# The last attention group of layer one: V's key block 7 in a bank of its own, and V, W_o and the first MLP load cut differently

## The chip, the core and the metric

The kernel runs on one core of one Trainium2 chip. The metric is the device time of one execution in microseconds; the median of three runs of the kernel before is 745.25 us (742.36 to 746.46). A core has a matrix engine (PE, with its weight loads shown as PEld), a vector engine (DVE), a scalar engine (ACT), GpSimd (POOL) and a sync engine (SP), which here only issues the loads. Matrix products are written to PSUM; everything else lies in SBUF, in 128 partitions.

## The reference

Two decoder layers, alternating attention and MLP, are run twice with the same weights on a batch of 4 with one token each, D = 640, all in f32:

```python
x = x + _A_ref(_layernorm(x), k_cache, v_cache, wq, wo)
x = x + _B_ref(_layernorm(x), W_gate, W_up, W_down)
x = x + _A_ref(_layernorm(x), k_cache, v_cache, wq, wo)
x = x + _B_ref(_layernorm(x), W_gate, W_up, W_down)
```

`_A_ref` takes 32 heads of 128, the last W = 1024 keys of the cache, and computes softmax(q k^T / sqrt(128)) v and then the product with wo. `_B_ref` computes (relu(x W_gate) * (x W_up)) W_down with F = 1728. Each batch row has its own K and V, so nearly all of the work is reading them.

## The kernel before

All weights and both caches lie in one HBM tensor, `stream`, of 128 partitions, in the order in which the first layer uses them. SBUF holds one large tile, `store`, of 55,040 columns of 4 bytes. One column of a load is 128 x 4 = 512 bytes. The list `todo` names the loads in order, with their sizes; `load()` goes through it, and puts a load on SP's queue as soon as the program has reached the point where the columns that it overwrites have been read for the last time. So the sizes in `todo` set both how much has to land before the matrix engine may go on, and how early the next load can be put into the freed place.

The 32 heads go in 8 groups of 4. For a group, `scores` (L272) multiplies q with K into the tile `ps` (two banks, four batch rows at partitions 0, 32, 64, 96), `softmax` (L279, L281) writes `probs`, `turned` (L296, L297) turns these into `pT`, and `values` (L305) multiplies `pT` with V into `po`. V is laid out by key block: 8 blocks of 128 keys, and for each block 4 heads of 512 columns (4 batch rows of 128). In `po`, head h has partitions 32h to 32h+3, each row b with the product of its probabilities with every batch row's V; only the piece where both are the same row is wanted. ACT copies `po` to `gates` (L308), four small matrix products (L314) turn the wanted pieces into `ms`, DVE scales them to `oT` (L317), and `project` (L325) multiplies with the group's rows of W_o into `yy`, which also gathers the residual.

Usually the turning and projecting of a group is done while the next group's K is landing. After the last group of a layer there is no next group: the turn, the projection, the layer norm (`normalized`, L201 to L220), and the first gate products of the MLP (`gate(3)`, L377) stand one behind the other. The layer norm's variance goes on beside these products.

The last group's K, V and W_o of layer one, group 7, are kept in SBUF for layer two, which starts with that group. While they are kept, the loads of layer one's MLP have only the last 6,912 columns of `store` to go round in (`RING`, from column `KEPT`). The first 6,528 of them (the first five MLP loads) fill places that earlier groups have long left. The sixth, and every one after it, waits until the matrix engine has read the place that it goes to: the sixth, 1,024 columns, for the first MLP load of 1,152 columns, which is the first 9 of the 15 steps of `gate(3)`.

`warm` is a product whose result is not read; it only keeps the matrix engine at work. The code before calls it twice during the last softmax, once after the last block of V, and between the MLP's products.

Of the kernel before, what the change touches and what calls it, by code (L numbers as in the profile page):

```python
# [12 lines left out]
B, D, H, DH, W, F = 4, 640, 32, 128, 1024, 1728  # L13
P = 128
# [7 lines left out]
GH = 4  # L22
G = H // GH
WQ, KV, WO = KC * GH * P, GH * 4096, GH * D
# [3 lines left out]
WD0 = GU0 + 3 * GU  # L28
TAIL, WD1, WD = WD0 + D, WD0 + D + 2 * QUARTER, 4 * D
# [3 lines left out]
AT = {}  # L33
# [21 lines left out]
M0 = AT["mlp"]  # L55
# [4 lines left out]
FRONT = VKEPT + WO  # L60
# [7 lines left out]
def decode_kernel(ctx: ExitStack, tc: tile.TileContext, x, stream, sel, out):  # L68
    nc = tc.nc
# [26 lines left out]
    run(0, AT["q", 7], AT["q", 7] + WQ, place=FRONT)  # L96
    run(0, AT["v", 6], vsplit)
    run(0, vsplit, AT["k", 7], place=0)
    steps(0, AT["k", 7], *[4096] * 7, 2048, 1024, 1024, 1280, 1280, place=FRONT + WQ)
    todo.append([KEPT])  # L100
    steps(0, M0, 9 * P, 6 * P, *[1536] * 3, 1024, 768, *[1536] * 5, 1280, WD1 - WD0, 2 * D, 3 * D, 3 * D, 2 * D, D, D)
    steps(1, AT["q", 6], 512, 1536, 512)
    steps(1, AT["k", 6], 2048, 2048)
    todo.append([FRONT, 0])
# [42 lines left out]
    def get(layer, lo, n):  # L147
        for first, m, p in held[layer]:
            if first <= lo and lo + n <= first + m:
                return store[:, p + lo - first:p + lo - first + n]  # L150
        raise KeyError((layer, lo, n))

    def done(layer, lo, n):
        if layer == 0 and any(a <= lo < b for a, b in kept):
            return
        for first, m, p in held[layer]:
            a, b = max(lo, first) - first, min(lo + n, first + m) - first
            if a < b:
                live[p + a:p + b] = [False] * (b - a)
        load()  # L160
# [4 lines left out]
    probs = work.tile([P, W], F32, name="probs")  # L165
    gates = work.tile([P, 512], F32, name="gates")
# [14 lines left out]
    po = psum.tile([P, 512], F32, name="po")  # L181
# [52 lines left out]
    def warm(moving=None):  # L234

        m = ident if moving is None else moving
        t = ps_p.tile([P, 512], F32, tag="p", name="unread")
        nc.tensor.matmul(t[:, :m.shape[-1]], ident, m, start=True, stop=True)  # L238
# [58 lines left out]
            nc.vector.tensor_copy(t[:, 4 * j:4 * j + 4], pp.rearrange("p c (b r) -> p c r b", r=32)[:, :, :GH, :])  # L297
        return t

    def values(layer, g, t, last):  # L300

        for c in range(8):
            for h in range(GH):
                lo = AT["v", g] + (c * GH + h) * 512
                nc.tensor.matmul(po[32 * h:32 * h + B], t[:, c, h], get(layer, lo, 512),  # L305
                                 start=c == 0, stop=c == 7, tile_position=(0, 32 * h))
                done(layer, lo, 512)
        nc.scalar.copy(gates, po)  # L308
        if last:
            warm(probs[:, :256])  # L310

    def values_turned(r):
        for b in range(B):
            nc.tensor.matmul(ms[:, b * GH:b * GH + GH], gates[:, b * P:(b + 1) * P], ident[:, b:P:32],  # L314
                             start=True, stop=True)
        oT = small.tile([P, GH, B], F32, name="oT")
        nc.vector.tensor_tensor(oT, ms[:, :GH * B].rearrange("p (b h) -> p h b", h=GH),  # L317
                                r.rearrange("p (h b) -> p h b", b=B), op=ALU.mult)
        return oT

    def project(layer, g, oT, last):
        for h in range(GH):
            for q in range(4):
                lo = AT["o", g] + h * D
                nc.tensor.matmul(y[32 * q:32 * q + B], oT[:, h], get(layer, lo + q * QUARTER, QUARTER),  # L325
                                 start=False, stop=last and h == GH - 1, tile_position=(0, 32 * q))
            done(layer, lo, D)

    def attention(layer, gs):
        load()  # L330
        xT, d = normalized()
        rs = []
        query(layer, gs[0], xT, lambda: rs.append(deviation(d)))
        rstd = rs[0]
        table(AF.Exp)
        query_out(rstd)
        query_turned()
        before = None
        for g, after in zip(gs, gs[1:] + [None]):
            scores(layer, g, 0)  # L340
            if before is None:
                go_on()
            else:
                project(layer, before, values_turned(r), False)
            for h in range(1, GH):
                scores(layer, g, h)
            sums = softmax()
            if after is not None:
                query(layer, after, xT)
                query_out(rstd)  # L350
# [9 lines left out]
            values(layer, g, t, layer == 0 and after is None)  # L360
            before = g
        project(layer, before, values_turned(r), True)


    def forward(layer):
# [135 lines left out]
```

## Time and profile before

| what | value |
|---|---|
| median of three runs | 745.25 us (742.36 to 746.46) |
| profiled execution, its own time | 742.0 us |
| its span, first to last instruction | 740.2 us |
| mean granted clock of the matrix engine | 0.808 |
| read from HBM | 312.37 MB, 422 GB/s over the span |
| matrix products, busy | 487.1 us of 740.2 |
| vector engine, scalar engine, busy | 59.0 us, 42.2 us |
| loads on SP's queue | 104 |

The times of the table's first row are without a profile; the profiled execution is one more. The span leaves out 1.8 us before and after the program's own instructions. The busy time of an engine is an average over all stages; which of them matters has to be read from the stretch around the change, which lies at about 340 to 380 us of the span.

### The profile page before, as it was taken

The page shows a single profiled execution, that of the slowest core. Times are in us where ns is not written, and L with a number is a line of the kernel's source. Part 1 is how long each engine was busy: PE and PEld are TensorE (multiplying, and loading weights), DVE is VectorE, ACT ScalarE, POOL GpSimd, SP SyncE. Part 2 cuts the span into 40 slices and gives each one's busy share as a digit, 9 for nine tenths or more (in the row PEclk, how much of TensorE's full clock was granted, in tenths as well). Part 3 has the DMA queues.
Part 4 walks back from the last instruction along what each step waited for, and adds up shares of the span by engine and source line. Part 5 has one row for each costly group of instructions (what it writes and reads, how often), then busy time and mean ns, then how long its engine had stood idle before and what let it go on. Part 6 is the DMA issues. An engine that isn't in the chain of part 4 may idle for free.

```text
span 740.2 us, 8264 instructions
## 1 busy us (share of the span) xinstructions
PE 487.1 (66%) x3844; PEld 158.5 (21%) x3844; DVE 59.0 (8%) x159; ACT 42.2 (6%) x74; POOL 0.2 (0%) x4
## 2 busy tenths in 40 slices
PE   3657376655855565767687997555666587576595
PEld 1112112212211121312233232111122022222142
DVE  2000100101010010101001110101001000010110
ACT  2000000000000000001001000000000000000100
POOL 0000000000000000000000000000000000000000
PEclk9978687876787777878999999778868678698777
DMA  9999999999999999999999999999999999999996
GB/s 388 425 452 437 414 438 433 420 453 414 447 424 427 444 418 416 443 419 425 412 377 402 425 438 426 429 421 443 428 431 437 427 438 429 427 432 433 406 429 284
DMA packets 15306, 312.99 MB, mean 423 GB/s; under 512 B 1700, under 2 KB 1956, under 8 KB 6824
## 3 DMA queue, kind: packets, MB, share of 16 engines
q1 hardware_dynamic: 15120, 312.37, 99.0%
q8 instruction: 30, 0.49, 0.3%
q10 hardware_dynamic: 152, 0.09, 0.0%
q14 instruction: 4, 0.03, 0.0%
HBM read 312.37 MB, written 0.08 MB: 422 GB/s over the span
## 4 chain that ended last, share of the span: by engine, by line
DMA 78%; PE 18%; another core or an unknown queue 2%; DVE 1%; issue 0%; SPq 0%; ACT 0%; ACTq 0%
DMA store<-in_stream 78%; PE ps L272 6%; PE po L305 4%; PE yy L325 2%; PE ms L314 2%; PE qp L252 1%; PE ms L263 1%; PE pp L296 0%; PE qp L377 0%; PE po L377 0%; SPq L143 0%; PE yy L409 0%; PE unread L238 0%; DVE oT L317 0%
## 5 line engine op out<-in xcount | busy, mean ns | idle before, releaser
L272 PE MATMUL ps<-store,qz 128*4 128x512 f32 x1024 | 168.3, 717 | 97.1 <-DMA store<-in_stream 96.6
L305 PE MATMUL po<-store,pT 128*4 128x512 f32 x1024 | 163.6, 745 | 83.7 <-DMA store<-in_stream 83.7
L272 PEld LDWEIGHTS ps<-store,qz 128*4 128x4 f32 x1024 | 30.7, 96 | 205.0 <-issue 112.3
L305 PEld LDWEIGHTS po<-store,pT 128*4 128x4 f32 x1024 | 28.5, 98 | 199.6 <-issue 110.0
L252 PE MATMUL qp<-store,xT 128*4 128x512 f32 x160 | 41.1, 760 | 26.7 <-DMA store<-in_stream 26.6
L281 ACT ACTIVATE probs<-ps,nm 128x1024 f32<-128x1024 f32 x16 | 17.8, 1113 | 308.7 <-DVE nm L279 308.7
L279 DVE TENSOR_REDUCE nm<-ps 128x1 f32<-128x1024 f32 x16 | 19.6, 1225 | 191.1 <-PE ps L272 191.1
L317 DVE TENSOR_TENSOR oT<-ms,r 128x16 f32<-128x16 f32 x16 | 2.8, 174 | 346.0 <-PE ms L314 346.0
L325 PE MATMUL yy<-store,oT 128*4 128x160 f32 x512 | 25.5, 351 | 4.3 <-DVE oT L317 4.3
L308 ACT COPY gates<-po 128x512 f32<-128x512 f32 x16 | 9.4, 585 | 309.3 <-PE po L305 309.3
L314 PEld LDWEIGHTS ms<-sel_sb,gates 128*128 128x128 f32 x128 | 18.7, 225 | 19.0 <-issue 16.8
L377 PE MATMUL po<-store,xT 128*4 128x256 f32 x160 | 17.2, 495 | 6.3 <-DMA store<-in_stream 6.1
L314 PE MATMUL ms<-sel_sb,gates 128*128 128x4 f32 x128 | 20.1, 281 | 0.9 <-ACT gates L308 0.8
L296 PE MATMUL pp<-sel_sb,probs 128*128 128x128 f32 x128 | 19.0, 296 | 0.0
L263 PE MATMUL ms<-sel_sb,gates 128*128 128x4 f32 x128 | 17.3, 258 | 1.7 <-DVE gates L257 1.7
L263 PEld LDWEIGHTS ms<-sel_sb,gates 128*128 128x128 f32 x128 | 17.3, 210 | 4.5 <-DVE gates L257 4.4
L252 PEld LDWEIGHTS qp<-store,xT 128*4 128x4 f32 x160 | 6.4, 96 | 50.4 <-DMA store<-in_stream 30.3
L296 PEld LDWEIGHTS pp<-sel_sb,probs 128*128 128x128 f32 x128 | 17.0, 166 | 0.0
L325 PEld LDWEIGHTS yy<-store,oT 128*4 128x4 f32 x512 | 13.4, 96 | 11.0 <-DVE oT L317 5.7
L285 PE MATMUL ms<-sel_sb,sm 128*128 128x16 f32 x32 | 7.0, 294 | 13.3 <-ACT probs L281 13.3
L257 DVE TENSOR_SCALAR gates<-qp,rstd 128x512 f32<-128x512 f32 x16 | 12.0, 749 | 41.6 <-PE qp L252 41.6
L285 PEld LDWEIGHTS ms<-sel_sb,sm 128*128 128x128 f32 x32 | 5.4, 210 | 31.5 <-ACT probs L281 24.9
(64 smaller groups left out, 115.2 us busy)
## 6 DMA issues: line engine op xcount, KB each, us to landing
store<-in_stream SPq DMA_DIRECT2D x26, 6656.0 KB, 50.2
store<-in_stream SPq DMA_DIRECT2D x11, 2048.0 KB, 32.3
store<-in_stream SPq DMA_DIRECT2D x2, 6784.0 KB, 51.0
store<-in_stream SPq DMA_DIRECT2D x6, 1280.0 KB, 20.7
store<-in_stream SPq DMA_DIRECT2D x7, 1024.0 KB, 8.5
store<-in_stream SPq DMA_DIRECT2D x9, 768.0 KB, 6.9
store<-in_stream SPq DMA_DIRECT2D x1, 6848.0 KB, 47.2
store<-in_stream SPq DMA_DIRECT2D x1, 6720.0 KB, 46.7
```

The source lines that it names most:

```text
L252: nc.tensor.matmul(qp[q:q + B], xT[:, c], get(layer, lo, GH * P), start=c < 4, stop=c > 0, tile_position=(0, q))
L257: nc.vector.tensor_scalar(gates, qp, rstd, SCALE, op0=ALU.mult, op1=ALU.mult)
L263: nc.tensor.matmul(ms[:, h * B:h * B + B], gates[:, h * P:(h + 1) * P], sel_b, start=True, stop=True)
L272: nc.tensor.matmul(ps[32 * b:32 * b + GH, j, :], qz[:, turn[0], b, GH * h:GH * h + GH], get(layer, lo, 512), start=h == 0, stop=h == GH - ...
L279: nc.vector.tensor_reduce(nm, flat, axis=AX.X, op=ALU.max, negate=True)
L281: nc.scalar.activation(probs, flat, AF.Exp, bias=nm, accum_out=sums)
L285: nc.tensor.matmul(ms[:, :GH * B].rearrange("p (h b) -> p h b", b=B), sums.to_broadcast([P, P]), ident_hb, start=True, stop=True)
L296: nc.tensor.transpose(pp[:, c, :], probs[:, (4 * j + c) * P:(4 * j + c + 1) * P], ident)
L305: nc.tensor.matmul(po[32 * h:32 * h + B], t[:, c, h], get(layer, lo, 512), start=c == 0, stop=c == 7, tile_position=(0, 32 * h))
L314: nc.tensor.matmul(ms[:, b * GH:b * GH + GH], gates[:, b * P:(b + 1) * P], ident[:, b:P:32], start=True, stop=True)
L325: nc.tensor.matmul(y[32 * q:32 * q + B], oT[:, h], get(layer, lo + q * QUARTER, QUARTER), start=False, stop=last and h == GH - 1, tile_pos ...
L377: nc.tensor.matmul(gu[32 * g:32 * g + B, :2 * n], xT[:, c], get(layer, lo, 2 * n), start=c == 0, stop=c == KC - 1, tile_position=(0, 32 * g))
```

## The change

Three things are changed, all in layer one's last group and the start of its MLP.

The loads: V's third load of 4,096 columns (key blocks 4 and 5) becomes two of 2,048, the second W_o load of 1,280 columns becomes two of 640 (one head's rows each), and the first two MLP loads of 1,152 and 768 columns become 768 and 1,152. Two later MLP loads of 1,024 and 768, which go round into their places, change order in the same way.

The products with V: `values` does seven of the eight key blocks into `po`. Both halves of `po` are then copied, one by DVE and one by ACT. Key block 7 goes, head by head and batch row by batch row, into the first bank of `ps` (free by then), where row b of each head is at partition 32b, so each product has 128 columns in place of 512. The turn of `po` stands between the block's first two heads and its last two. The heads of block 7 are copied to `probs`, one each by ACT and DVE, and four more turning products add them to `ms`. The unread product after the last V block is gone. The same code serves the other groups and layer two through the old path.

```diff
-    steps(0, AT["k", 7], *[4096] * 7, 2048, 1024, 1024, 1280, 1280, place=FRONT + WQ)
+    steps(0, AT["k", 7], *[4096] * 6, 2048, 2048, 2048, 1024, 1024, 2 * D, D, D, place=FRONT + WQ)
     todo.append([KEPT])
-    steps(0, M0, 9 * P, 6 * P, *[1536] * 3, 1024, 768, *[1536] * 5, 1280, WD1 - WD0, 2 * D, 3 * D, 3 * D, 2 * D, D, D)
+    steps(0, M0, 6 * P, 9 * P, *[1536] * 3, 768, 1024, *[1536] * 5, 1280, WD1 - WD0, 2 * D, 3 * D, 3 * D, 2 * D, D, D)
...
-    def values(layer, g, t, last):
+    def values(layer, g, t, blocks=8):
...
-        nc.scalar.copy(gates, po)
-        if last:
-            warm(probs[:, :256])
+        if blocks < 8:
+            nc.vector.tensor_copy(gates[:, 256:], po[:, 256:])
+            nc.scalar.copy(gates[:, :256], po[:, :256])
+        else:
+            nc.scalar.copy(gates, po)
+
+    def last_values(layer, g, t):
+
+        values(layer, g, t, 7)
+        for hs in (0, 1), (2, 3):
+            for h in hs:
+                lo = AT["v", g] + (7 * GH + h) * 512
+                for b in range(B):
+                    nc.tensor.matmul(ps[32 * b:32 * b + B, 0, h * P:(h + 1) * P], t[:, 7, h],
+                                     get(layer, lo + b * P, P), start=True, stop=True, tile_position=(0, 32 * b))
+                done(layer, lo, 512)
+            for h, copy in zip(hs, (nc.scalar.copy, nc.vector.tensor_copy)):
+                copy(probs[:, h * P:(h + 1) * P], ps[:, 0, h * P:(h + 1) * P])
+            if hs[0] == 0:
+                turn_values(more=True)
...
+    def values_turned(r, last=False):
+        if last:
+            for h in range(GH):
+                nc.tensor.matmul(ms[:, h:GH * B:GH], probs[:, h * P:(h + 1) * P], ident[:, 0:P:33],
+                                 start=False, stop=h == GH - 1)
+        else:
+            turn_values()
```

What the matrix engine executes at this place, from the last group's softmax to the layer norm. Each row is a run of equal products of one line, with the written and read tiles, the columns written, and how many. Before:

```order
L238 MATMUL unread<-gates,sel_sb 128x512 x2
L285 MATMUL ms<-sel_sb,sm 128x16
L296 MATMUL pp<-sel_sb,probs 128x128 x8
L305 MATMUL po<-store,pT 4x512 x32
L238 MATMUL unread<-probs,sel_sb 128x256
L314 MATMUL ms<-sel_sb,gates 128x4 x4
L325 MATMUL yy<-store,oT 4x160 x16
L208 MATMUL xt_ps<-sel_sb,probs 128x16
```

And with the change, where L331 is the old L314, L350 the old L325, L321 the products of key block 7 and L337 their turn:

```order
L238 MATMUL unread<-gates,sel_sb 128x512 x2
L285 MATMUL ms<-sel_sb,sm 128x16
L296 MATMUL pp<-sel_sb,probs 128x128 x8
L305 MATMUL po<-store,pT 4x512 x28
L321 MATMUL ps<-store,pT 4x128 x8
L331 MATMUL ms<-sel_sb,gates 128x4 x4
L321 MATMUL ps<-store,pT 4x128 x8
L337 MATMUL ms<-sel_sb,probs 128x4 x4
L350 MATMUL yy<-store,oT 4x160 x16
L208 MATMUL xt_ps<-sel_sb,probs 128x16
```

The last four of 32 wide products became sixteen narrow ones, the turn of `po` moved ahead of the last eight of them, and a second turn of four products came in behind.

On SP's queue, the loads from group 7's K to the MLP's first half, with their columns. Before:

```order
L143 DMA store<-in_stream 128x4096 x7
L143 DMA store<-in_stream 128x2048
L143 DMA store<-in_stream 128x1024 x2
L143 DMA store<-in_stream 128x1280 x2
L143 DMA store<-in_stream 128x1152
L143 DMA store<-in_stream 128x768
L143 DMA store<-in_stream 128x1536 x3
L143 DMA store<-in_stream 128x1024
L143 DMA store<-in_stream 128x768
L143 DMA store<-in_stream 128x1536 x5
```

With the change:

```order
L143 DMA store<-in_stream 128x4096 x6
L143 DMA store<-in_stream 128x2048 x3
L143 DMA store<-in_stream 128x1024 x2
L143 DMA store<-in_stream 128x1280
L143 DMA store<-in_stream 128x640 x2
L143 DMA store<-in_stream 128x768
L143 DMA store<-in_stream 128x1152
L143 DMA store<-in_stream 128x1536 x3
L143 DMA store<-in_stream 128x768
L143 DMA store<-in_stream 128x1024
L143 DMA store<-in_stream 128x1536 x5
```

There are two loads more, 106 in place of 104, of the same columns in all.

More of the change, by code (lines that the diff above doesn't have):

```diff
@@ L298, in turned @@
         return t
-    def values(layer, g, t, last):
-        for c in range(8):
+    def values(layer, g, t, blocks=8):
+        for c in range(blocks):
             for h in range(GH):
@@ L305, in values, with turn_values @@
                 nc.tensor.matmul(po[32 * h:32 * h + B], t[:, c, h], get(layer, lo, 512),
-                                 start=c == 0, stop=c == 7, tile_position=(0, 32 * h))
+                                 start=c == 0, stop=c == blocks - 1, tile_position=(0, 32 * h))
                 done(layer, lo, 512)
-        nc.scalar.copy(gates, po)
-        if last:
-            warm(probs[:, :256])
-    def values_turned(r):
+        if blocks < 8:
[16 more added lines that the diff above has]
+                turn_values(more=True)
+    def turn_values(more=False):
         for b in range(B):
             nc.tensor.matmul(ms[:, b * GH:b * GH + GH], gates[:, b * P:(b + 1) * P], ident[:, b:P:32],
-                             start=True, stop=True)
+                             start=b == 0, stop=b == B - 1 and not more)
+    def values_turned(r, last=False):
[5 more added lines that the diff above has]
+            turn_values()
         oT = small.tile([P, GH, B], F32, name="oT")
@@ L359, in attention @@
                 query_turned()
-            values(layer, g, t, layer == 0 and after is None)
+            last = layer == 0 and after is None
+            (last_values if last else values)(layer, g, t)
             before = g
-        project(layer, before, values_turned(r), True)
+        project(layer, before, values_turned(r, last), True)
     def forward(layer):
```

## The prediction

> **What bounds the kernel now.** I read the page first, its DMA line and the chain that ended last:
>
> ```profile
> span 740.2 us, 8264 instructions
> DMA  9999999999999999999999999999999999999996
> HBM read 312.37 MB, written 0.08 MB: 422 GB/s over the span
> DMA 78%; PE 18%; another core or an unknown queue 2%; DVE 1%; issue 0%; SPq 0%; ACT 0%; ACTq 0%
> ```
>
> The 16 DMA engines are at 90% or more in all slices but the last, and the chain is loads for 78%. 18% on PE means only that some loads were issued when PE gave a place free; whether the queue ran dry meanwhile must be read from landings. So I looked at the timeline of PE around the change, where a row that waits for a load starts as the load lands:
>
> ```profile
> 338.50 2.54 PE L272 MATMUL ps<-store,qz 128*4 128x512 f32 x16 [2.39 <-DMA store<-in_stream]
> 343.41 3.38 PE L272 MATMUL ps<-store,qz 128*4 128x512 f32 x16 [2.37 <-DMA store<-in_stream]
> 353.21 1.90 PE L305 MATMUL po<-store,pT 128*4 128x512 f32 x16 [0.61 <-DMA store<-in_stream]
> 358.23 1.90 PE L305 MATMUL po<-store,pT 128*4 128x512 f32 x16 [3.12 <-DMA store<-in_stream]
> 360.65 1.04 PE L305 MATMUL po<-store,pT 128*4 128x512 f32 x8 [0.52 <-DMA store<-in_stream]
> 361.93 1.03 PE L305 MATMUL po<-store,pT 128*4 128x512 f32 x4 [0.24 <-DMA store<-in_stream]
> 363.19 1.03 PE L305 MATMUL po<-store,pT 128*4 128x512 f32 x4 [0.24 <-DMA store<-in_stream]
> 364.15 0.70 PE L238 MATMUL unread<-probs,sel_sb 128*128 128x256 f32 x2
> 369.27 1.16 PE L377 MATMUL qp<-store,xT 128*4 128x128 f32 x27
> 372.52 1.03 PE L377 MATMUL po<-store,xT 128*4 128x256 f32 x12 [0.86 <-DMA store<-in_stream]
> 374.43 1.03 PE L377 MATMUL po<-store,xT 128*4 128x256 f32 x12 [0.87 <-DMA store<-in_stream]
> 375.70 0.60 PE L377 MATMUL po<-store,xT 128*4 128x256 f32 x4 [0.24 <-DMA store<-in_stream]
> ```
>
> 4,096 columns take 4.91 us (338.50 to 343.41), 1,024 take 1.26 (361.93 to 363.19). That is (4.91 - 1.26) / 3,072 = 1.19 ns a column and 1.26 - 1.22 = 0.04 us for each load; with the 1.28 from 360.65 to 361.93 in place of 1.26 it is 1.18 ns and 0.07 us. In the MLP, behind the transition, the pace is the same: 1,536 columns in 1.91 us (1.81 + 0.07 = 1.88), then 1,024 in 1.27. So loads land without a gap before, over and behind the transition.
>
> Now the chain there, from V's last landing to the first load that had to wait for PE:
>
> ```profile
> 363.19 1.05 PE po L305 x4
> 364.32 0.59 ACT gates L308
> 364.96 1.07 PE ms L314 x8
> 366.05 0.19 DVE oT L317
> 366.28 1.31 PE yy L325 x32
> 367.68 0.30 ACT probs L201
> 368.02 0.40 PE xt_ps L208 x2
> 369.27 0.85 PE qp L377 x17
> 370.14 5.51 DMA store<-in_stream
> 375.65 0.04 issue
> ```
>
> SP issues the sixth MLP load (1,024 columns) at 370.14 and it lands at 375.65. What would be the earliest? The kernel's first load, on an empty queue, from the list of issues:
>
> ```profile
> store<-in_stream SPq DMA_DIRECT2D x1, 1280.0 KB, 5.6
> ```
>
> 1,280 KB are 2,560 columns, 3.02 us at 1.18 ns, so 2.6 us are latency. The sixth MLP load could have landed at 370.14 + 2.6 + 1.21 = 373.95. It landed 1.7 us later, because it stood behind the loads ahead of it: **the long serial chain has 1.7 us to spare**. One view speaks against this, the windows:
>
> ```profile
> 360.00:370.00 10.00, 8.04 (x103) 3.90 (x102) 1.24 (x6) 0.88 (x2) 0.00 (x0) 1.00 1.02 415
> 370.00:374.00 4.00, 2.64 (x47) 1.07 (x41) 0.44 (x2) 0.57 (x2) 0.00 (x0) 1.00 0.91 335
> 374.00:384.00 10.00, 9.02 (x83) 3.38 (x83) 0.86 (x4) 0.73 (x2) 0.00 (x0) 1.00 1.01 382
> 384.00:394.00 10.00, 8.11 (x96) 3.11 (x93) 0.43 (x2) 0.37 (x1) 0.00 (x0) 1.00 1.02 403
> ```
>
> The last three columns are granted clock, DMA share and GB/s. In 370 to 374 the DMA share is 0.91 and the rate falls from 415 to 335: some of the 16 engines do run dry. But a load has landed only when its slowest engine is done, and the landings above (1.91, 1.27) show no gap. My reading: the engines that are ahead run dry, the one that is behind does not, and it sets the time.
>
> **The change, part by part.**
>
> *Two more loads.* V's blocks 4 and 5 in two, W_o's second load in two: 2 x 0.04 to 0.07 us, +0.1 us, on the path, because the queue is the bound. SP's own time to issue them hides: the chain has SPq at 0%. The Trainium skill, "DMA: Bandwidth & Descriptors", section "Anatomy of one DMA", fits about 2.0 us of fixed cost to each DMA (on the GpSimd path); two more would be an estimated +4.0 us by that, 746.0 in place of 742.1. The landings here show the fixed part overlapped when loads queue behind each other, and I take the row.
>
> *Key block 7.* Before, the last two heads take 1.05 us, ACT's copy 0.59, the turn 1.07. With the change the last two heads are eight products of 128 columns, one quarter of the columns in four groups: the 1.90 us of a full block pair (16 records of 512) divided by 4 is 0.5. From the other side, 27 records of 128 columns (`gate(3)`) took 1.16 us, so 16 take 0.7. I take 0.6. The copies of 128x128 are one each on ACT and DVE; the nearest rows are
>
> ```profile
> L201 ACT COPY probs<-yy x4: 292/292/292, 11.8 to 710.6; 128x160 f32<-128x160 f32 x4
> L297 DVE COPY pT<-pp x32: 160/224/226, 47.4 to 691.4; 128x64 f32<-128x64 f32 x32
> ```
>
> so 0.3 us for the later of the two. Of the second turn's four products the first two run during these copies; the last two cost half of 1.07, 0.5. The turn of `po` (1.07 us) moves ahead, but not for free: block 6 lands at 360.65, is done at 361.7, its two half copies end near 362.1, the first half of block 7 ends about 362.5, the turn then at 363.6, 0.4 us behind V's last landing at 363.2. That is what queues there: the last eight products wait for the turn. So the last products run 363.6 to 364.2, copies to 364.5, turn to 365.1, `oT` and its hand-overs (366.28 - 366.03 = 0.25) to 365.3: the projection may start 1.0 us earlier than 366.28.
>
> *W_o is late next.* Its last columns follow V's by 2,560 columns, 3.0 us, plus three loads' fixed cost: 366.4. Two thirds of the projection and more are done by then; only the last head's four products (a quarter of 1.31, 0.33) follow. It ends at 366.8 in place of 367.6: **0.8 us gained on PE, not 2**. The unread product that is taken out cost nothing: it ran from 364.15 to 364.85, beside ACT's copy.
>
> *The first MLP load of 768 columns.* It is read in 6 of 15 steps, so its place is free after 0.57 in place of 0.85 us. The sixth MLP load is then issued at 370.14 - 0.8 - 0.3 = 369.05, **1.1 us earlier**. It lands behind the same queue as before. Worth on the path: 0 as long as the 1.7 us of cover stand; if the cover had been gone, at most 1.1 us. V's block 4 lands and is read earlier, which is also hidden.
>
> *Engines that run dry later or not at all.* The engines ahead keep up to 1.1 us more of their lead, and a lead is of use when something delays one engine. Such a thing is on the page:
>
> ```profile
> q8 instruction: 30, 0.49, 0.3%
> ```
>
> 30 fetches of instructions are 0.3% of 16 engines' span, 740.2 x 16 x 0.003 / 30 = 1.2 us of one engine each. One or two of them fall in the next 20 us; a kept lead could hide one wholly or not at all, 0 to 1.1 us. MLP loads go round in 6,912 columns (8.2 us), so the lead is cut again within these; I take 0.2. The change adds some 70 instructions to 8,264, a quarter of a fetch by 8,264 / 30 = 275 for each: 0 to +1.2, I take 0.
>
> Sum: +0.1 - 0.2 = -0.1 us on the profiled execution's 742.0 us (span 740.2 and 1.8 around it), which is no change. That execution is 3.25 us under the median of the runs, inside their spread of 4.1. I put the same sum on the median: **745.2 us**. Half a per cent, 3.7 us, is about what a measurement of this kernel can tell from no change.
>
> **The rivals.**
>
> 1. *The dry engines count.* If what all 16 engines move sets the time, the stretch 370 to 394 lacks (415-335)/415 x 4 + (415-382)/415 x 10 + (415-403)/415 x 10 = 1.9 us, and the 1.1 us earlier issue wins back most of its share: 1.1 us, 744.2. For it: the windows. Against: evenly spaced landings. Also within half a per cent.
>
> 2. *The transition stalls in runs without a profile.* The median is 3.25 us over the profiled run, and if all of that were a stall at this place, through a PE clock that fell before the last V blocks, the finer V loads would keep PE at work and take it away with the 1.1 us: 745.25 - 4.3 = 741.0, faster. For it: the clock does fall near here, as in
>
> ```profile
> 340.00:344.00 4.00, 1.63 (x12) 0.11 (x8) 0.00 (x0) 0.00 (x0) 0.00 (x0) 0.50 0.98 418
> ```
>
> and the row at 343.41 takes 3.38 us for what takes 1.90 at full clock. Against: the window 360 to 370 has clock 1.00, and 3.1 us of waiting before 358.23 did not lower it.
>
> 3. *Slower: the clock falls in the MLP.* An unread product is gone, and the products with V are a quarter as wide, so PE does less between 361 and 367. At half clock (3.38 against 1.90, 1.78 times) the chain's 4 us of PE work take 3 us more, and the issue at 369.05 becomes 372.1, past 370.14 + 1.7 = 371.85: from there it decides, with 0.3 us. Then the second and third gate products, 10,240 columns with an unread one behind each 1,024, need 0.55 + 0.42 = 0.97 us for each 1,024 at full clock, by the chain's
>
> ```profile
> 377.10 0.55 PE qp L377 x8
> 377.65 0.42 PE unread L238 x2
> ```
>
> and 1.7 at half, against landings of 1.27: 0.45 x 10 = 4.5 us if the clock stays low through both, with the 0.3 us 4.8 us, about 750; half of it, if the clock recovers midway, 748. Against: the pieces land 1.3 to 2.5 us apart, closer than the 5.0 before (353.21 to 358.23), so PE has no longer pause than now. The Trainium skill, "TensorE: Matmul & The Clock Gate", says the clock is lowered after an idle window of about 3.4 us; by that rule the change makes this less likely, and the 3.1 us pause that kept full clock agrees.
>
> **How the numbers follow.** Hidden, no change, 745.2: 0.62 (744 to 746.4 by the unknown costs). Dry engines count, 744.2: 0.24. Stall removed, 741.0: 0.08. Clock falls, 748 and over: 0.06. Faster by over half a per cent takes the third case and not all of it, slower nearly all of the last: 0.07 and 0.05, within it 0.88. The runs before spread from 742.4 to 746.5 by themselves, more than any term of the sum, so the range takes their spread around 745.2 and stretches to case 3's lower half: 742.0 to 747.8.
>
> **What would show it.** In the changed profile: V's last landing to the next rows' loads at the same spacing (1.9 us for 1,536 columns); the projection's last quarter waiting for W_o, and the layer norm about 0.8 us earlier relative to V's last landing; SP's first waiting MLP load about 1.1 us earlier, its time to landing longer by the same (5.5 to about 6.6) and the landing not earlier; a DMA share in the four microseconds around it nearer to 1.0 than 0.91. I am wrong if landings behind the transition come earlier by as much as the chain does, if PE's granted clock leaves 1.00 between 360 and 394, or if the time moves by more than 3.7 us.

## The result: slower by half a per cent, and the profile after

| | before | after |
|---|---|---|
| median of 22 runs each | 746.54 us (742.36 to 749.1, and one of 970.31) | 750.39 us (743.9 to 754.26) |
| ratio after / before | | 1.0053, 95% interval 1.0032 to 1.0074 |
| profiled execution | 742.0 us, clock 0.808 | 751.56 us, clock 0.801 |

The changed kernel is slower by 3.9 us. The forecast of no change (745.2, 742.0 to 747.8) is wrong, and what came is its third rival. The profiled run of before is faster than every one of its 22 runs, that of after slower than after's median: the two profiles lie 9.5 us apart, the medians 3.9. The first lines of the page after, its DMA line, what it read and its chain:

```profile
span 749.8 us, 8334 instructions
DMA  9999999999999999999999999999999999999996
HBM read 312.37 MB, written 0.08 MB: 417 GB/s over the span
DMA 77%; PE 20%; DVE 1%; another core or an unknown queue 1%; issue 0%; SPq 0%; ACT 0%; ACTq 0%; DVEq 0%
```

The bytes are the same, the rate is 417 GB/s in place of 422, and PE has two points more of the chain. The page does not say where. The windows do: clock, DMA share and GB/s are the last three columns. First before, then after:

```profile
364.00:374.00 10.00, 7.68 (x126) 4.67 (x124) 1.69 (x8) 1.45 (x4) 0.00 (x0) 1.00 0.98 385
374.00:390.00 16.00, 14.73 (x126) 5.38 (x127) 0.86 (x4) 0.73 (x2) 0.00 (x0) 1.00 1.01 389
390.00:405.00 15.00, 11.28 (x168) 5.47 (x168) 2.59 (x10) 2.41 (x5) 0.00 (x0) 1.00 1.02 406
```

```profile
364.00:374.00 10.00, 9.21 (x130) 6.04 (x126) 1.98 (x9) 1.13 (x4) 0.00 (x0) 0.58 0.93 356
374.00:390.00 16.00, 13.33 (x103) 5.19 (x99) 0.86 (x4) 0.74 (x2) 0.00 (x0) 0.73 0.93 342
390.00:405.00 15.00, 11.20 (x134) 4.89 (x130) 0.61 (x3) 0.37 (x1) 0.00 (x0) 0.83 0.96 354
```

Before, PE keeps its full clock through all three stretches. After, it has 0.58, 0.73 and 0.83 of it, and the transfer rate falls with it, from 385 to 356 and from 389 to 342. PE's timeline after, from V's last blocks into the gate products:

```profile
355.74 1.04 PE L305 MATMUL po<-store,pT 128*4 128x512 f32 x8 [0.68 <-DMA store<-in_stream]
358.14 1.04 PE L305 MATMUL po<-store,pT 128*4 128x512 f32 x8 [1.36 <-DMA store<-in_stream]
360.65 1.04 PE L305 MATMUL po<-store,pT 128*4 128x512 f32 x8 [1.48 <-DMA store<-in_stream]
361.92 0.62 PE L321 MATMUL ps<-store,pT 128*4 128x128 f32 x16 [0.22 <-DMA store<-in_stream]
362.72 1.05 PE L331 MATMUL ms<-sel_sb,gates 128*128 128x4 f32 x8 [0.18 <-ACT gates L310]
363.70 0.62 PE L321 MATMUL ps<-store,pT 128*4 128x128 f32 x16
364.25 1.17 PE L337 MATMUL ms<-sel_sb,probs 128*128 128x4 f32 x8
365.68 2.32 PE L350 MATMUL yy<-store,oT 128*4 128x160 f32 x32 [0.27 <-DVE oT L342]
370.11 2.10 PE L403 MATMUL qp<-store,xT 128*4 128x128 f32 x27
372.33 4.09 PE L403 MATMUL po<-store,xT 128*4 128x256 f32 x39
379.84 0.61 PE L403 MATMUL qp<-store,xT 128*4 128x256 f32 x6 [1.13 <-DMA store<-in_stream]
382.94 1.02 PE L403 MATMUL qp<-store,xT 128*4 128x256 f32 x2 [1.54 <-DMA store<-in_stream]
384.62 1.04 PE L403 MATMUL qp<-store,xT 128*4 128x256 f32 x8
385.58 0.80 PE L238 MATMUL unread<-sel_sb 128*128 128x128 f32 x2
386.31 1.03 PE L403 MATMUL qp<-store,xT 128*4 128x256 f32 x8
```

Up to 365.68 all is at full speed: the last eight products start at 363.70 (forecast 363.6), the projection at 365.68 (forecast 365.3, before 366.28). Then the projection takes 2.32 us in place of 1.27, 27 gate products 2.10 in place of 1.16, and the 39 records from 372.33 run as one block of 4.09 with no wait for a load, where before there were three waits: PE is behind the queue now. Later it waits 1.13 and 1.54 us: the queue has run out. The projection before, in the same view:

```profile
366.28 1.27 PE L325 MATMUL yy<-store,oT 128*4 128x160 f32 x32 [0.27 <-DVE oT L317]
```

The list of landings gives the whole loss. From each landing's distance to the one before I take 1.18 ns a column and 0.07 us for the load, and call the rest, where it is over 0.05 us, a gap:

| profiled run | time | gaps, whole span | of them at landings from 365 to 495 us | time less gaps |
|---|---|---|---|---|
| before | 742.0 | 7.3 | 2.4 | 734.7 |
| after | 751.56 | 16.8 | 12.0 | 734.7 |

All of the 9.5 us between the two profiled runs is gaps in 365 to 495, that is the MLP of layer one and the start of layer two. From 340 to 365 there is none over 0.05 us. The same holds for the experiments: time less gaps lies between 734.7 and 735.6 us in all 18 profiled runs.

One of the gaps shows how it comes. SP's first waiting load is issued at 371.19 (before 370.14), still inside its 1.7 us of cover: it lands without a gap. Those behind it are issued up to 2.5 us later than the same columns before (374.24 in place of 371.70), and the engines use up their lead: before, the first of the 16 pieces of the load landing at 376.63 was 2.2 us ahead of the last; after, 0.54 us (the load landing at 376.68). Then the last pieces of two loads come late, 1.55 and 2.75 us behind the first ones, and the two take 6.2 us to land (376.68 to 382.90) in place of 3.8. In that stretch there is a fetch of instructions, at 379.3; the line for it in the DMA queues of after, 370 to 385 us (packets, MB, share of 16 engines):

```profile
q8 instruction: 1, 0.02, 0.4%
```

### The profile page after: what moved, and what is told of

It reads as the page before. It is cut to its first block, busy times and chain, and to the rows that moved or that the text cites. A ratio compares the mean times of both kernels' runs of the same rounds, so it can differ in the third digit from the quotient of the medians.

```text
span 749.8 us, 8334 instructions
## 1 busy us (share of the span) xinstructions
PE 492.2 (66%) x3874; PEld 163.4 (22%) x3874; DVE 60.3 (8%) x162; ACT 42.5 (6%) x76; POOL 0.2 (0%) x4
## 4 chain that ended last, share of the span: by engine, by line
DMA 77%; PE 20%; DVE 1%; another core or an unknown queue 1%; issue 0%; SPq 0%; ACT 0%; ACTq 0%; DVEq 0%
DMA store<-in_stream 77%; PE ps L272 6%; PE po L305 4%; PE yy L350 2%; PE ms L331 2%; PE qp L252 1%; PE unread L238 1%; PE po L403 1%; PE qp L403 1%; PE yy L435 1%; PE ms L263 1%; PE pp L296 1%; SPq L143 0%; DVE oT L342 0%
## 5 line engine op out<-in xcount | busy, mean ns | idle before, releaser
L272 PE MATMUL ps<-store,qz 128*4 128x512 f32 x1024 | 171.3, 732 | 102.9 <-DMA store<-in_stream 102.3
L305 PE MATMUL po<-store,pT 128*4 128x512 f32 x1016 | 158.2, 732 | 78.6 <-DMA store<-in_stream 78.6
L252 PE MATMUL qp<-store,xT 128*4 128x512 f32 x160 | 39.6, 728 | 23.7 <-DMA store<-in_stream 23.6
L350 PE MATMUL yy<-store,oT 128*4 128x160 f32 x512 | 27.6, 372 | 4.3 <-DVE oT L342 4.3
L331 PEld LDWEIGHTS ms<-sel_sb,gates 128*128 128x128 f32 x128 | 20.5, 244 | 20.2 <-issue 18.0
L331 PE MATMUL ms<-sel_sb,gates 128*128 128x4 f32 x128 | 21.9, 295 | 1.0 <-ACT gates L312 0.8
L403 PE MATMUL po<-store,xT 128*4 128x256 f32 x160 | 14.5, 506 | 6.2 <-DMA store<-in_stream 6.2
L350 PEld LDWEIGHTS yy<-store,oT 128*4 128x4 f32 x512 | 13.8, 100 | 12.2 <-DVE oT L342 5.7
L403 PE MATMUL qp<-store,xT 128*4 128x256 f32 (+1 forms) x140 | 11.4, 393 | 5.0 <-DMA store<-in_stream 4.8
```

The costliest lines, as they stand in the source:

```text
L252: nc.tensor.matmul(qp[q:q + B], xT[:, c], get(layer, lo, GH * P), start=c < 4, stop=c > 0, tile_position=(0, q))
L272: nc.tensor.matmul(ps[32 * b:32 * b + GH, j, :], qz[:, turn[0], b, GH * h:GH * h + GH], get(layer, lo, 512), start=h == 0, stop=h == GH - ...
L403: nc.tensor.matmul(gu[32 * g:32 * g + B, :2 * n], xT[:, c], get(layer, lo, 2 * n), start=c == 0, stop=c == KC - 1, tile_position=(0, 32 * g))
```

## The theories

*Clock*: PE's clock falls in the transition or behind it, PE gives places free late, the loads' gaps are the loss. *Fetches*: the 70 instructions more move the fetches to where they hurt. *Loads*: the finer loads cost more than 0.04 to 0.07 us each. And a question inside the first: which edit lets the clock fall, the missing unread product, the narrow products, or the finer V loads?

## The experiments: which part of the change

The first four ran together, and each was timed against before in 12 runs.

**After, with two unread products behind block 7.** They stand ahead of the second turn, where the removed one had been.

```diff
             (last_values if last else values)(layer, g, t)
+            if last:
+                warm()
+                warm()
```

> The changed kernel with two unread 128-column products put back between the last product of key block 7 and its turn (together as many columns as the one that the change took out). Clock theory: PE does so little between 361 and 366 us that its granted clock falls to 0.5 at 365.7, and everything behind it runs at half speed; with the unread products the clock stays 1.00 from 347 to beyond 400, the first waiting MLP load is issued near 370 and no MLP load lands late: ratio to the kernel before 0.998 to 1.002. If two are too little, the clock still falls and the ratio stays near 1.005. Load theory: the two more loads and the other cut make the queue run dry whatever the clock does: still 1.004 to 1.007.

Ratio 1.0054 (1.0032 to 1.0075): nothing is won back. Its profiled run, 748.5 us, does hold the clock in the transition, and so shows the new chain at full speed:

```profile
363.92 0.62 PE L321 MATMUL ps<-store,pT 128*4 128x128 f32 x16
364.47 0.71 PE L238 MATMUL unread<-sel_sb 128*128 128x128 f32 x4
365.02 0.95 PE L337 MATMUL ms<-sel_sb,probs 128*128 128x4 f32 x8
366.24 1.27 PE L350 MATMUL yy<-store,oT 128*4 128x160 f32 x32 [0.27 <-DVE oT L342]
369.23 1.16 PE L406 MATMUL qp<-store,xT 128*4 128x128 f32 x27
```

```profile
369.89 0.33 SPq L143 DMA_DIRECT2D store<-in_stream  x1
```

The unread ones put 0.55 us on the chain (364.47 to 365.02). V's last load landed at 363.40 here, so without them the issue is at 369.89 - 0.55 - 363.40 = 5.94 us behind V; the forecast was 369.05 - 363.15 = 5.90. There is a fetch at 379.7, in the same place as after's, but the two loads that took 6.2 us after take 3.8 here, with leads of 2.2 to 2.8 us; the load behind them is 0.89 us late. The clock, which was expected to hold beyond 400, falls from 397.4 to 404.2, in the down products:

```profile
390.00:405.00 15.00, 11.37 (x144) 5.23 (x136) 1.12 (x5) 0.66 (x2) 0.00 (x0) 0.77 0.92 337
```

and the gaps of 365 to 495 are 8.6 us. So the loss is not tied to one place.

**Before, with the changed loads alone** (the two lines of `steps` of the diff above).

> The kernel before with only the changed loads (V's blocks 4 and 5, W_o and the first MLP loads cut as in the change), products as before with the unread one. Clock theory: the products keep the clock as before, ratio 0.998 to 1.002; if it is the shorter pauses between V's blocks that let the clock fall, about 1.004. Load theory: all of the loss is here, 1.004 to 1.007.

1.0011 (0.9993 to 1.0029). Two more loads at 2.0 us each, the Trainium skill's fixed cost (on the GpSimd path) in "DMA: Bandwidth & Descriptors", section "Anatomy of one DMA", would be an estimated 4.0 us or 1.0054, outside this interval. The loads theory falls as the whole cause.

**Before's loads, after's products.** `last_values` and the second turn as in the diff above (so without the unread product), `steps` as before.

> The changed products (key block 7 in its own bank, its own turn, without the unread product), the loads cut as before. Clock theory: nearly all of the loss is here, 1.003 to 1.007, with the granted clock falling to 0.5 between 361 and 370. Load theory: 0.998 to 1.002.

1.0026 (0.9999 to 1.0054): some of the loss perhaps; not settled by itself.

**Before without its unread product.**

```diff
         nc.scalar.copy(gates, po)
-        if last:
-            warm(probs[:, :256])
```

> The kernel before without the one unread product behind the last block of V, nothing else changed. Clock theory in its narrow form (that product alone kept the clock): 1.003 to 1.006 and a clock that falls near 365. In its wide form (the narrower products matter as much): 1.000 to 1.003. Load theory: 0.999 to 1.001, since nothing about the loads is changed.

1.0009 (0.9987 to 1.0031). Its profiled run, 747.96 us, has half clock from 359.9 to 363.3 and from 366.7 to 373.5, although by its runs the kernel is hardly slower than before. With the first experiment, which put products back and won nothing, the missing product is not shown to be the cause by itself.

## The experiments: fetches or clock

Small unread products (128x4) at the start of the program move all later instructions, and with them the fetches. They also raise the mean clock over the span (0.816 in the first kernel below, before beside it 0.808), so mean clocks of kernels with and without them are not compared here.

```diff
+    t = ps_p.tile([P, 512], F32, tag="p", name="unread")
+    for _ in range(16):
+        nc.tensor.matmul(t[:, :4], ident, ident[:, :4], start=True, stop=True)
     attention(0, list(range(G)))
```

**Before with 16 of them.** The fetch at 384.1 moves to 379.7.

> The kernel before with 16 tiny unread products (128x4) at its start, where PE waits for the first loads. They are 64 more PE instructions, as many as the change adds, so that every later fetch of instructions comes as early in the program as in the changed kernel; nothing else is changed. Fetch theory (the change is slower because a fetch moves from 384 us, between two gate products, to 379.5, where it delays a DMA engine that is already behind): about 1.003 to 1.005, with the fetch near 379.5. Clock theory (what PE streams in each 3.4 us around the last V block and the MLP's start sets the granted clock): 0.999 to 1.001.

0.9991 (0.9970 to 1.0011). **After with its two unread products behind block 7, and 46 small ones:**

> The first experiment (the changed kernel with two unread products put back) with 46 tiny products at the start, so that with its own 72 more instructions the fetches are moved by 256, one whole fetch, and fall where they do in the kernel before (384, not 379.5). Fetch theory: 0.999 to 1.002, and no loss of a load between 380 and 400. Clock theory: unchanged, about 1.005.

1.0038 (1.0014 to 1.0063). **After with 48 small ones and nothing else:**

> The changed kernel with 48 tiny products at the start, so that fetches fall where they do in the kernel before; the unread product behind the last V block stays out. Fetch theory alone: 0.999 to 1.002. Clock theory alone: about 1.005, with a clock of 0.5 within 358 to 372. Both together: 1.002 to 1.004.

1.0033 (1.0007 to 1.0060). Before does not become slower, nor is after shown to be as fast as before, where the fetches lie elsewhere. The profiles say the same of single loads: in before with 16 small products the loads from 376 to 385 us land without a gap over the fetch at 379.7, and in after with 48 one load lands 2.14 us late (377.88 to 381.90) with no fetch from 373.2 to 382.8. So fetches alone are not it; what held up the last pieces in after's two late loads is not shown, and a small part of the time for the fetches is not excluded.

**After with PE kept at work at every wait**: two unread products behind each of V's blocks 3 to 6, four behind block 7, one more place in the down products, and 36 small ones at the start.

```diff
                 done(layer, lo, 512)
+            if blocks < 8 and c > 2:
+                warm()
+                warm()
...
+            if last:
+                warm()
+                warm()
+                warm()
+                warm()
...
-                if layer == 0 and j == 1:
+                if layer == 0 and j < 2:
                     warm()
```

> The changed kernel with more unread products: two behind each of V's blocks 3 to 6, four behind block 7, and one in each step of the MLP's down product that had none, with 36 tiny products at the start so that fetches fall as before. Clock theory: every 3.4 us window from 347 to 400 then streams enough, the granted clock stays 1.00 there, and the ratio is 0.995 to 0.999. If the unread products themselves get in the way of real ones: over 1.002 with the clock at 1.00.

0.9991 (0.9971 to 1.0012), with a mean clock of 0.820 over its runs (0.815 in after with 48 small ones): the loss is gone, with after's loads and after's products. Its interval and after's do not touch. The clock was not held as expected, though: its profiled run, 748.33 us and so one of its slower ones, has 1.00 from 342 to 369.3 and half clock from 369.3 to 372.7 and from 396.6 to 403.5.

## The experiments: the cover, and how wide the unread products must be

**Before, with four more unread products of 512 columns behind the last block of V.** This makes the chain longer, to measure the cover of 1.7 us.

```diff
             warm(probs[:, :256])
+            for _ in range(4):
+                warm(probs[:, :512])
```

> The kernel before with four more unread products of 512 columns behind the last V block: about 3.7 us more on the serial chain, at full clock, since they stream. The prediction's cover (1.7 us between the first waiting MLP load's earliest and its real landing): the load is issued near 373.8 and lands 3.7 - 1.7 = 2.0 us behind its place in the queue; ratio near 1.002. All hidden: no gap. Nothing hidden (the chain is on the path in full): a gap of 3.7 us, ratio 1.005.

1.0044 (1.0026 to 1.0062). SP's first waiting load, and the windows:

```profile
374.29 0.33 SPq L143 DMA_DIRECT2D store<-in_stream  x1
```

```profile
364.00:374.00 10.00, 9.20 (x92) 5.60 (x91) 1.24 (x6) 0.88 (x2) 0.00 (x0) 0.89 0.79 320
```

Relative to V's last landing (363.40 here, 363.15 before) the issue is 3.90 us later, partly because the clock fell here too. The load lands 3.20 us behind the one before it (374.61 to 377.81) where 1,024 columns take 1.28, a gap of 1.92: the cover was 3.90 - 1.92 = 2.0 us. The forecast had 1.7. The ratio is above the 1.002 expected; the clock fell again from 371.8 to 378.6, so the ratio is not the price of the four products alone. Here the DMA engines stand idle for want of a free place, and a share of 0.79 shows it.

**After, with one unread product of 512 columns behind block 7:**

```diff
+            if last:
+                warm(gates)
```

> The changed kernel with one unread product of 512 columns behind key block 7, twice the columns of the one taken out, nothing else. Clock theory with one place (the thin stretch from V's last landing to the projection): clock 1.00 from 347 to 390 and a ratio of 0.999 to 1.002, against 1.005 with 256 columns. If the shorter pauses between V's blocks or the down product matter as much: 1.002 to 1.004.

1.0059 (1.0032 to 1.0086). A wide product there does not help more than two narrow ones, and in its profiled run the clock, expected at 1.00 from 347 to 390, falls from 360.0 to 363.5, from 370.3 to 373.7 and from 383.9 to 387.3. The next two go back to **before's products, with after's loads**, the unread ones behind V's blocks 3 to 6, 512 columns in place of 256 behind block 7, and the additional place in the down products:

```diff
+            if last and 2 < c < 7:
+                warm()
+                warm()
         nc.scalar.copy(gates, po)
         if last:
-            warm(probs[:, :256])
+            warm(probs[:, :512])
...
-                if layer == 0 and j == 1:
+                if layer == 0 and j < 2:
```

> The kernel before with the change's loads and more unread products: two behind each of V's blocks 3 to 6, 512 columns in place of 256 behind block 7, one in each step of the down product that had none. Clock theory: the same as the changed products with unread ones in these places (0.9991), 0.996 to 0.999, which says that block 7's new form costs nothing by itself when the clock holds. If the new form costs time by itself (a second turn, narrow products): lower than that by 0.002 or more.

0.9991 (0.9972 to 1.0009); its profiled run has half clock from 369.1 to 372.5 and from 396.4 to 403.3. **The same with still more of them**, in the down products and behind layer two's first softmax:

> The one before with still more unread products: a second one in every other step of the down product, and two behind the first softmax of layer two, where the clock fell in nearly every profile (396 to 404, 410 to 414). Clock theory: 0.994 to 0.998, and fewer stretches at 0.5 between 395 and 420. If PE is full there: 0.999 to 1.002.

1.0000 (0.9985 to 1.0015). The fastest forms, with either kind of products, are as fast as before and not faster.

## The experiments: which wait matters

The kernel with all unread products had won back everything; these four take it apart. All are after with one or two of the edits shown.

**Only the two behind each of V's blocks 3 to 6:**

> The changed kernel with two unread products behind each of V's blocks 3 to 6 and nothing else. If it is the pauses between V's blocks that let the clock fall: 0.999 to 1.002, clock 1.00 up to 362 at least. If it is the thin stretch from V's last landing to the projection: still 1.003 to 1.006, with a clock that falls between 362 and 371.

1.0012 (0.9995 to 1.0030), below after's interval; its profiled run has full clock from 341.7 to 369.0. **Only the one in the down products:**

> The changed kernel with one unread product in each of the MLP's down steps that had none (one of layer-one's four parts more), nothing else. If what brought the time back before was the down product: 0.999 to 1.002. If it was what stands ahead of the MLP: 1.004 to 1.006.

1.0077 (1.0049 to 1.0106). Its profile shows the chain at half clock nearly from end to end:

```profile
358.23 1.58 PE L305 MATMUL po<-store,pT 128*4 128x512 f32 x8 [1.35 <-DMA store<-in_stream]
360.75 1.89 PE L305 MATMUL po<-store,pT 128*4 128x512 f32 x8 [0.94 <-DMA store<-in_stream]
363.66 1.87 PE L331 MATMUL ms<-sel_sb,gates 128*128 128x4 f32 x8 [0.17 <-ACT gates L310]
366.43 1.87 PE L337 MATMUL ms<-sel_sb,probs 128*128 128x4 f32 x8
368.56 2.31 PE L350 MATMUL yy<-store,oT 128*4 128x160 f32 x32 [0.27 <-DVE oT L342]
```

```profile
374.07 0.33 SPq L143 DMA_DIRECT2D store<-in_stream  x1
```

The clock is 0.5 from 358.6 to 375.7. Ahead of the fall V's pieces were the only work, 1.04 us in each 2.5. Both turns take 1.87 us. The first waiting load is issued 10.8 us behind V's last landing (before 7.0), past the cover, with a gap of 1.78 us at its landing.

**The ones behind V's blocks and one of 512 columns behind block 7:**

> The changed kernel with two unread products behind each of V's blocks 3 to 6 and one of 512 columns behind block 7. If V's pauses and the thin stretch act together: 0.997 to 1.001, clock 1.00 from 347 to 369 at least. If the down product's unread ones were needed too: 1.002 to 1.004.

1.0024 (1.0004 to 1.0045): by its twelve runs a part of the loss remains. But the profiled one, the fastest of them, is 742.82 us, nearly as short as before's, and shows what the changed kernel does when the clock stands:

```profile
364.00:374.00 10.00, 7.84 (x136) 4.76 (x128) 1.98 (x9) 1.13 (x4) 0.00 (x0) 1.00 1.01 393
374.00:390.00 16.00, 14.17 (x126) 5.36 (x127) 0.86 (x4) 0.75 (x3) 0.00 (x0) 1.00 1.00 388
390.00:405.00 15.00, 11.04 (x168) 5.38 (x168) 2.59 (x10) 2.39 (x5) 0.00 (x0) 1.00 1.01 401
```

Clock 1.00 in all three rows, transfer rates as before (385, 389, 406), gaps of 2.4 us in 365 to 495 and 7.4 in all; 742.82 less 7.4 is 735.4.

**After without the unread products of the gate steps:**

```diff
-                if layer == 0 and j in (1, 2):
-                    warm()
```

> The changed kernel without the unread products of the MLP's second and third gate products. If a low clock costs time because at half speed 1,024 columns take 1.04 us of products and 0.80 of unread ones, more than the 1.27 us in which they land: 0.999 to 1.003, although the clock is lower than before. If they keep up the clock there, and that is worth more: over 1.006.

1.0037 (1.0018 to 1.0055), between the two forecasts. Whether these help the clock or only cost PE time is undecided: the interval overlaps after's.

Taken together: of the kernels with block 7 in its own form and after's loads, those with unread products in the waits for V have 0.9991, 1.0012 and 1.0024, those without 1.0033 to 1.0077. Over the 22 runs of after time and mean granted clock go against each other (correlation -0.78; the fastest, 743.9 us, has 0.808, the slowest, 754.26, has 0.788). In before, with 33 to 35 runs beside each set of experiments, the tie is weaker (-0.01 to -0.53). Among the kernels with after's products and loads and no small products at the start, the mean clock goes with the time too: it is 0.801 to 0.805 where the ratio is 1.0037 to 1.0077, and 0.809 and 0.810 where it is 1.0012 and 1.0024; before has 0.809 to 0.812 beside them. With small products at the start it shows less: 0.815 in after at 1.0033, 0.816 in before at 0.9991.

## Why the prediction was wrong

*The step that failed* is the third rival's "Against: the pieces land 1.3 to 2.5 us apart, closer than the 5.0 before, so PE has no longer pause than now", and with it the chance of 0.06: on the strength of it the sum takes the clock as full throughout and has no term for it. The length of the pauses alone does not decide here. The clock changes in steps of 3.41 us, so each such stretch can be looked at by itself. Before, two of them, both followed by full clock:

```profile
353.33:356.74 3.41, 1.78 (x16) 0.21 (x8) 0.00 (x0) 0.00 (x0) 0.00 (x0) 1.00 0.96 405
356.74:360.15 3.41, 1.90 (x16) 0.36 (x16) 0.00 (x0) 0.00 (x0) 0.00 (x0) 1.00 0.99 402
```

After, the two that lie ahead of the fall at 365.7:

```profile
358.90:362.30 3.40, 1.70 (x28) 0.43 (x24) 0.42 (x1) 0.01 (x1) 0.00 (x0) 1.00 1.01 404
362.30:365.70 3.40, 2.95 (x46) 2.36 (x38) 0.76 (x3) 0.89 (x3) 0.00 (x0) 1.00 1.03 408
```

PE is busy for 1.78 us before and keeps its clock; it is busy for 2.95 us after, with 46 records and no pause over 0.2 us but the 0.27 for `oT` at its end, and loses it. What differs is what streams through: 16 records of 512 columns before; narrow products of 128 and turns of 4 columns after.

Nor did the 3.1 us pause ahead of 358.23 show that such a pause is safe. In before's profile a step of the clock ends at 356.74, in the middle of it. In before with 16 small products, whose V loads and products are the same, the steps lie otherwise, and one of them holds most of the pause. Its line and the next:

```profile
355.90:359.30 3.40, 0.60 (x8) 0.25 (x12) 0.00 (x0) 0.00 (x0) 0.00 (x0) 1.00 1.00 410
359.30:362.80 3.50, 3.50 (x23) 0.55 (x14) 0.00 (x0) 0.00 (x0) 0.00 (x0) 0.51 1.02 415
```

The clock falls at 359.3. That it held in before's profile was, by this pair, the luck of where the steps lay. The fall did no harm at the first waiting load, which is issued at 371.25 and lands without a gap (the run took 745.92 us).

The rule of an idle window of about 3.4 us, which the prediction took from the Trainium skill, "TensorE: Matmul & The Clock Gate", has the right length but not the right condition for the row at 362.30; the measurement decides.

*What was right in that rival*: its direction, and its price in sum. It gave 748 to 750; the median is 750.4. Half-clock gate products with their unread ones were put at 1.7 us for 1,024 columns; after's rows are 1.69 apart (384.62 to 386.31). *What was wrong in it*: it named the missing unread product as the first reason, which by itself shows nothing (1.0009), and put the loss into the second and third gate products (4.5 us) and 0.3 for the late issue. After's issue at 371.19 stayed within the cover, and the gaps spread over 100 us, from 379.8 to 487.7, over the rest of the MLP and into layer two. The leads are back at 1.7 us by 402; but the clock falls again and again, from 382.8 to 389.6, 399.8 to 406.7, 413.5 to 416.9, 427.1 to 430.5 and 461.3 to 471.5. So the loss is not where the price put it, and that the sum came out near it is luck.

*The sum, term by term.* Two more loads, +0.1: not contradicted (1.0011, and no gap over 0.05 us from 340 to 365). The chain at full clock, issue 1.1 us earlier: 5.94 us behind V against 5.90. One term in it was mis-sized: the second turn, put at 0.5 because two of its products would run beside the copies, took 0.95 to 1.17, and the projection was 0.6 us earlier in place of 1.0. W_o landed at 366.4 as forecast (its first half of two at 365.57, and 0.83 us for 640 columns), but the projection did not have to wait for it in the run at full clock (1.27 us, as before). Cover 1.7: 2.0. "Worth on the path: 0": the fast forms with the new loads (0.9991 with the new products, 0.9991 and 1.0000 with the old) agree. So with unread products in V's waits the change is worth what was forecast, nothing; what was left out of the sum is what it does to the clock without them.

*The second rival* pointed at something real. The 742.0 us of before's profile was better than all its other runs: the median over 22 is 746.54, and other kernels close to before show falls of the clock too, in the transition (before with 16 small products, above; before without its unread product) or behind it (the loads alone: 403.5 to 413.7, with gaps of 9.0 us in 365 to 495, in a run of 747.78). So the kernels before and after may differ only in how often and how long the clock falls, and one profile of each cannot tell that. The finer V loads alone did not make the kernel faster (1.0011).

*Still open.* How the 0.53% is split: the loads alone have 1.0011, the missing product alone 1.0009, the missing product and the narrow ones together 1.0026. Loads and products add up to 1.0037, inside the interval of the whole change, but each of the three intervals reaches 1.0; and the narrow products with before's loads and an unread one were not run. Why a fall may come at 365 in one run and only at 397 in the next: the 3.41 us steps do not start with the program (before it changes at 346.5 + n x 3.41, after at 341.8 + n x 3.41), which would make it chance. The fall at 359.3 above agrees; it was not tested by runs made for it.

## What to carry to other kernels

In a kernel that waits for its loads, an edit to a serial stretch has to be judged at both clocks of the matrix engine: work out the chain at full and at half clock, and set both against the cover of the first load that waits for it. Where narrow products took the place of wide ones, the clock fell behind a stretch in which PE looked busier; whether finer loads do so too is not shown. Unread products in the waits ahead of the chain brought the time back here (1.0012), some inside it did not (1.0054 and 1.0059). And a single profiled run of a kernel with a spread of 1% may be its best one: ask what its other runs lose before adding to it.

## What the runs showed of the hardware

In all 18 traces the granted clock changes only in steps of 3.41 us. I counted, for each such stretch at full clock, the columns of all product records (each f32 product leaves two), each weighted by how many quarters of the 128-wide array its weights take up (a product with 4 rows of output counts a quarter). Under 800, the next stretch was at half clock in 513 cases of 513; over 1,500, in 1 of 1,495; between, in 197 of 280. After's stretch ahead of 365.7 has 765, before's at the same place 1,573; the one ahead of the fall at 358.6 in the kernel with one more product in the down steps has 1,283. This is a count fitted to these traces, not a rule tested on others.

At most 8 loads of SP's queue are under way: each further one was issued only as the load 8 before it had landed (after: the last block of V at 363.16, the load 8 behind it at 363.18). The loads carry eight semaphores in turn, so this can be a limit of the program; that it is one of the chip is not shown. And each of the 30 fetches of instructions, 0.49 MB in all, is one packet with a record of about 1 us. What a fetch costs is not shown: the two cases above are one without a gap over a fetch and one gap without a fetch.
